# Putting off small-tile visits by a count of TensorE's instructions, and dating layer A's probabilities later, in a two-layer attention kernel

## The chip, the core and the metric

One core of a Trainium2 chip runs the whole program. Its engines work from queues of their own: TensorE (PE, with its weight loads shown apart as PEld), VectorE (DVE), ScalarE (ACT), GpSimd (POOL) and SyncE (SP, here an issuer of DMAs). The metric is device time in microseconds for one execution; lower is better.

## The reference

Two attention layers, A and B, read inputs of 2048 rows by 1024 columns. Each multiplies by `wqkv` (1024 x 3072), attends with 32 heads of 32, and multiplies by `wo` (1024 x 1024); the outputs are put side by side. Only the attention differs.

```python
# A: each row sees 8 keys, two rows apart, itself among them
off = jnp.arange(W) * dil                     # W, dil = 8, 2
idx = pos[:, None] - off[None, :]
logits = jnp.einsum("bhsd,bhswd->bhsw", q, kg) * scale    # kg, vg: k, v gathered at idx
o = jnp.einsum("bhsw,bhswd->bhsd", softmax(where(idx >= 0, logits, -1e9)), vg)
# B: each row sees the last 256 keys
mask = (i - j >= 0) & (i - j < 256)
o = jnp.einsum("bhqk,bhkd->bhqd", softmax(where(mask, q @ k.T * scale, -1e9)), v)
```

## The kernel before

**Units and groups.** The work is eight units of 512 rows: units 0 to 3 are layer B, units 4 to 7 layer A, whose even and odd rows are laid apart so that its eight keys are neighbours. A unit has eight groups of four heads. The 32 groups of layer A are called visits 0 to 31 here; eight of them make a unit.

**Large matmuls.** The projections run on 128-wide tiles. Each fp32 operand is split into a high and a low fp32r part, and three products of parts (`TERMS`) replace one fp32 product. In the profile these are the matmuls `g<-...`: queries and keys (L586), values (L654), the output projection of layer B (L714), and that of layer A (L773), which is done with sums of blocks at the program's end.

**Layer A's small tiles.** A visit has two pieces of TensorE work. `scores` (L923) multiplies 64 pairs of 32x32 and 32x40 tiles into four PSUM banks. `values` (L984) multiplies 16 or 20 tiles of probabilities (`wide`) with values (`vbuf`) into one bank. The operands here are plain fp32, and each such matmul stands in the trace as two weight loads and two matmuls: 64 of them are 256 instructions. A large matmul is two.

**Between them** lies a chain on two other engines: VectorE adds the mask (L931), takes the maximum (L941) and subtracts it (L943); ScalarE takes the exponential (L947); VectorE sums (L955), inverts (L957), multiplies (L959) and turns the tiles (L961); ScalarE spreads them into `wide` (L970, L973, eight copies). Only then can `values` start. After it, ScalarE copies the result out (L1032).

**Loads.** Weights and inputs come through GpSimd's queue (L173) into raw buffers. ScalarE or VectorE makes the high part (L218, L221), VectorE the low part (L224). At the change of a unit the eight tiles of the next input, `x`, are loaded and split in four pairs.

**What sets the order.** Nothing is scheduled on the chip. While the program is built, a planner keeps a clock (`Clock`) with times for all engines and DMAs. There are four lists of work: `aux`, `twos` (values), `ones` (scores) and `gemm` (large matmuls, three at a time, in a fixed sequence). At each step the planner asks the next item of each list when it will be ready, takes the earliest, and emits it. Every engine's order follows from this, for the work that follows a TensorE item is emitted at the time at which the planner thinks it due. The chip then runs each engine's queue strictly in that order.

An item of `values` is ready when its `v` is, when a PSUM bank is, and when `h["p"]`, the planned end of the last copy into `wide`, has come:

```python
return latest(done["v"].get((u, vp)), h.get("p"), ro.when())
```

## Time and profile before

| | |
|---|---|
| median of 3 runs | 1819.04 us (1817.57 to 1820.43) |
| the profiled execution | 1818.1 us, of which the span is 1816.4 us |
| TensorE matmuls busy | 1789.4 us, 99% of the span, 14730 matmuls |
| VectorE, ScalarE, GpSimd busy | 1262.0, 924.4 and 410.1 us |
| layer A's `scores` (L923) | 43.3 us busy |
| layer A's `values` (L984) | 38.5 us busy |
| granted TensorE clock, mean | 0.995 of full speed |

A row of the timeline gives the start in us from the span's start, the length, engine, line, operation, tiles and count; in brackets is the idle time just before it and what ended that. "issue" means that the profile shows nothing that the engine waited for. The length of a run of matmuls ends with the modelled end of the last one, which overlaps the next start by about 0.07 us; differences of starts are the safer measure.

### The profile page before, as it was taken

The numbers are of one execution on the slowest core, as the hardware profiler recorded it, in microseconds if no ns is written. First come the engines' busy times: TensorE is split into PE (matmuls) and PEld (weight loads), VectorE is DVE, ScalarE is ACT, GpSimd is POOL, SyncE is SP. The second block draws the span as 40 slices with busy tenths as digits, with TensorE's granted clock in tenths as the row PEclk, the third lists the DMA queues.
The fourth block names the chain that finished last, engine by engine and source line by source line (L and its number), as shares of the span: only waits on it lengthen the run. The fifth ranks groups of instructions, "written<-read, shape, count | busy, mean of one in ns | idle before, by whom it ended". The sixth has DMA issues, their size and how long they took to land.

```text
span 1816.4 us, 38617 instructions
## 1 busy us (share of the span) xinstructions
PE 1789.4 (99%) x14730; PEld 1465.3 (81%) x14730; DVE 1262.0 (69%) x2790; ACT 924.4 (51%) x2301; POOL 410.1 (23%) x950
## 2 busy tenths in 40 slices
PE   9999999999999999999999999999999999999999
PEld 6787878888777788778887788888888887888887
DVE  6677876768867769777677566646755766557866
ACT  5556466555655565656555344423542544446342
POOL 2313323222242223333224300101010011002220
PEclk9999999999999999999999999999999999999999
DMA  7354664544646555454545343536753674348984
GB/s 239 114 142 136 183 168 139 167 139 137 183 139 177 146 144 170 134 166 128 160 110 164 106 150 119 164 123 213 249 173 113 221 250 137 120 144 297 311 265 145
DMA packets 129241, 303.61 MB, mean 167 GB/s; under 512 B 16160, under 2 KB 31520, under 8 KB 129056
## 3 DMA queue, kind: packets, MB, share of 16 engines
q0 software_dynamic: 45216, 164.65, 28.7%
q1 hardware_dynamic: 73472, 116.56, 22.8%
q10 hardware_dynamic: 10368, 19.93, 3.0%
q8 instruction: 117, 1.92, 0.4%
q14 instruction: 68, 0.56, 0.1%
HBM read 189.79 MB, written 44.04 MB: 129 GB/s over the span
## 4 chain that ended last, share of the span: by engine, by line
PE 91%; DMA 3%; ACT 2%; DVE 2%; issue 1%; SPq 0%; POOL 0%; ACTq 0%; DVEq 0%; POOLq 0%
PE g L586 37%; PE g L654 18%; PE g L714 10%; PE g L773 8%; PE s L1172 5%; PE s L1089 5%; PE o L1219 5%; PE s L923 2%; PE o L984 2%; DMA r<-od 2%; DMA raw<-xs 1%; ACT wide L970 1%; ACT s L1099 0%; DVE w L224 0%; DVE r L846 0%
## 5 line engine op out<-in xcount | busy, mean ns | idle before, releaser
L586 PE MATMUL g<-x,w 128*128 128x512 f32 x3072 | 773.0, 396 | 2.8 <-ACT x L218 2.6
L586 PEld LDWEIGHTS g<-x,w 128*128 128x128 f32 x3072 | 568.1, 189 | 114.5 <-issue 6.8
L654 PE MATMUL g<-w,x 128*128 128x256 f32 (+1 forms) x2304 | 393.7, 322 | 0.5 <-issue 0.3
L224 DVE TENSOR_TENSOR w<-raw,w 128x512 fp32r<-128x512 f32 x518 | 339.4, 697 | 51.8 <-ACT w L218 45.1
L654 PEld LDWEIGHTS g<-w,x 128*128 128x128 f32 x2304 | 334.5, 192 | 28.8 <-issue 1.6
L1099 ACT ACTIVATE s<-s,nm 128x384 f32<-128x384 f32 (+2 forms) x512 | 274.4, 537 | 101.8 <-DVE nm L1094 101.6
L1094 DVE CUSTOM_DVE_ANT_0 s<-s,mask_d 128x384 f32<-128x384 f32 (+2 forms) x512 | 261.7, 554 | 88.1 <-PE s L1089 87.4
L1158 POOL TENSOR_SCALAR_AFFINE_SELECT pbuf<-pbuf 128x128 f32<-128x128 f32 (+1 forms) x606 | 220.1, 391 | 326.2 <-ACT pbuf L1179 324.8
L1179 ACT ACTIVATE pbuf<-s 128x384 f32<-128x384 f32 (+2 forms) x480 | 202.8, 505 | 73.7 <-PE s L1172 72.1
L714 PE MATMUL g<-r,w 128*128 128x512 f32 x768 | 190.8, 394 | 1.4 <-ACT r L1054 0.7
L173 POOL DMA_DIRECT2D raw<-wqk x126 | 68.6, 545 | 440.8 <-DVE w L224 303.0
L714 PEld LDWEIGHTS g<-r,w 128*128 128x128 f32 x768 | 141.9, 188 | 30.7 <-DVE r L1058 1.6
L773 PE MATMUL g<-x,w 128*128 128x512 f32 x672 | 153.2, 390 | 0.5 <-DVE w L224 0.5
L773 PEld LDWEIGHTS g<-x,w 128*128 128x128 f32 x672 | 126.0, 188 | 27.3 <-DVE w L224 0.9
L221 DVE CAST w<-raw 128x1024 fp32r<-128x1024 f32 x187 | 129.3, 692 | 25.2 <-PE g L586 22.6
L1172 PEld LDWEIGHTS s<-qst,kst 128*128 128x128 f32 x704 | 113.3, 189 | 40.6 <-ACT s L1099 16.2
L1089 PE MATMUL s<-kst,qst 96*128 96x384 f32 (+2 forms) x512 | 142.5, 342 | 0.9 <-ACT s L1099 0.7
L1172 PE MATMUL s<-qst,kst 128*128 128x256 f32 (+2 forms) x704 | 136.4, 302 | 3.5 <-ACT s L1099 3.0
L1089 PEld LDWEIGHTS s<-kst,qst 96*128 96x128 f32 x512 | 93.5, 189 | 25.8 <-issue 3.9
L931 DVE TENSOR_TENSOR band<-s,near 128x160 f32<-128x160 f32 x128 | 32.5, 316 | 116.0 <-PE s L923 116.0
L1099 ACT ACTIVATION_READ_ACCUMULATOR s<-s,nm 128x1 f32 x512 | 105.4, 206 | 0.0
L970 ACT COPY wide<-band 32x512 f32<-32x512 f32 x128 | 79.0, 618 | 49.2 <-DVE band L961 47.2
(81 smaller groups left out, 1405.7 us busy)
## 6 DMA issues: line engine op xcount, KB each, us to landing
raw<-wqk POOLq DMA_DIRECT2D x126, 512.0 KB, 4.3
raw<-wv POOLq DMA_DIRECT2D x72, 512.0 KB, 4.9
qst<-nat SPq DMA_DIRECT2D x96, 256.0 KB, 5.4
kst<-nat SPq DMA_DIRECT2D x96, 256.0 KB, 5.5
raw<-wo POOLq DMA_DIRECT2D x44, 512.0 KB, 4.4
raw<-xs POOLq DMA_DIRECT2D x28, 512.0 KB, 4.5
outs<-ost ACTq DMA_DIRECT2D x37, 256.0 KB, 2.8
kst<-halo SPq DMA_DIRECT2D x72, 128.0 KB, 4.4
```

The lines of the kernel that those rows point to most:

```text
L221: nc.vector.tensor_copy(t[:, 0, :], raw)
L224: nc.vector.tensor_tensor(t[:, 1, c:c + 512], raw[:, c:c + 512], t[:, 0, c:c + 512].bitcast(F32), op=ALU.subtract)
L586: nc.tensor.matmul(h["ps"], h["w"][:, a, k * P:(k + 1) * P], xt[u][k][:, b, :], start=(k == 0 and i == 0), stop=(k == NK - 1 and i == 2))
L654: nc.tensor.matmul(ps, xt[u][kw * g + k][:, a, p0:p0 + P], h["w"][g][:, c, k], start=(first and t == 0 and half == 0), stop=(last and t == 2),
L714: nc.tensor.matmul(h["ps"], w[:, a, c:c + P], ot[u, k][:, b, :], start=(k == 0 and i == 0), stop=(k == NK - 1 and i == 2))
L773: nc.tensor.matmul(h["ps"], w[:, a, c:c + P], x[:, b, :], start=(k == 0 and t == 0), stop=(k == 3 and t == 2))
L1089: nc.tensor.matmul(ps[:, :n], q[0:96, j, b * P:(b + 1) * P], kk[0:96, j, c0:c1], start=True, stop=True)
L1094: nc.vector.tensor_tensor_reduce(ps[:, :n], ps[:, :n], mask[:, cut:full], scale=-1.0, scalar=BIG, op0=ALU.add, op1=ALU.min, accum_out=nm)
L1099: nc.scalar.activation(ps[:, :n], ps[:, :n], AF.Exp, bias=nm, scale=-1.0, accum_out=sm)
L1158: nc.gpsimd.affine_select(w, w, pattern=[[0, m], [step, n]], compare_op=ALU.is_ge, fill=0.0, base=base, channel_multiplier=chan)
L1172: nc.tensor.matmul(ps[:, i * n:(i + 1) * n], kk[:, j, 256 + kb * P:256 + (kb + 1) * P], q[:, j, q0:q0 + n], start=True, stop=True)
L1179: nc.scalar.activation(w, ps[:, :pack * n].rearrange("p (j n) -> p j n", j=pack), AF.Exp)
```

## The change

It has two parts, and both act only in the planner.

**The count.** A helper `mm` wraps each matmul and adds 4 (fp32) or 2 to a count of TensorE's instructions. Each time the count passes another 256, at an offset of 150, it notes the planner's time. It takes this as the moment at which TensorE asks for its next 256 instructions. `EXTRA` and `EACH` stand for instructions that the wrapped calls don't show. `short(n)` is true if an item of n instructions would run past the 290 that are still there at the asking, and less than 7.0 us of planned time have passed since. In the main loop an item of `scores` (256 instructions) or `values` (16 to 80) for which this holds is passed over for large matmuls, if those are ready within 0.2 us.

**The date.** The end of layer A's probabilities, `h["p"]`, is taken as 1.5 us later when the planner asks whether `values` is ready.

No work is added or removed. Where the planner finds ScalarE or VectorE free at another time, it hands a piece to the other: nine high parts of weights (L218) go from ScalarE to VectorE (L221), two high parts of inputs and three copies out of PSUM the other way. All matmuls now have one source line, L269, so tile names tell them apart.

```diff
+CHUNK, ASKED, LEFT, FETCHED = 256, 150, 290, 7.0
+EXTRA, EACH = 246, 5.2
+P_LATE = 1.5
...
+    issued, asked = [0.0], [0, 0.0]
+
+    def mm(out, left, right, **k):
+        issued[0] += 4 if left.dtype == F32 else 2
+        n = int(issued[0] + EXTRA - ASKED) // CHUNK
+        if n > asked[0]:
+            asked[:] = n, ck.now
+        nc.tensor.matmul(out, left, right, **k)
+
+    def short(n):
+        return ck.now < asked[1] + FETCHED and issued[0] + EXTRA + n > asked[0] * CHUNK + ASKED + LEFT
...
         def scores():
             qk = rows[hg]
+            issued[0] += EACH
...
-                        nc.tensor.matmul(banks[j][0][32 * i:32 * i + 32, 40 * b:40 * b + 40],
+                        mm(banks[j][0][32 * i:32 * i + 32, 40 * b:40 * b + 40],
...
-            return latest(done["v"].get((u, vp)), h.get("p"), ro.when())
+            return latest(done["v"].get((u, vp)), h.get("p") and h["p"] + P_LATE, ro.when())
...
-        return [Item(scores_ready, scores, CW)], [Item(values_ready, values, C3 + 0.9)]
+        return [Item(scores_ready, scores, CW, 256)], [Item(values_ready, values, C3 + 0.9, 16 * len(kbs))]
...
-        best = None
+        best, other = None, None
         left = False
         for name, seq in seqs.items():
...
             t = seq[pos[name]].ready()
+            if t is not None and name == "g" and t <= ck.now + 0.2:
+                other = max(t, ck.now), name
             if t is not None and (best is None or max(t, ck.now) < best[0]):
                 best = max(t, ck.now), name
+        if best and other and seqs[best[1]][pos[best[1]]].n and short(seqs[best[1]][pos[best[1]]].n):
+            best = other
```

TensorE's order is the same up to the first `scores` visit of layer A, 1043 us into the span, and in the closing run of large matmuls. In between, the places of the 32 `scores` and 32 `values` among the large matmuls move; the large matmuls keep their sequence.

**Place one: TensorE in unit 4, from the `scores` of visit 6 to the `values` of visit 7** (`s<-pbuf` is `scores`, `o<-wide,vbuf` is `values`, `g` the large matmuls). Before:

```order
L923 MATMUL s<-pbuf 32x40 x64
L586 MATMUL g<-x,w 128x512 x6
L654 MATMUL g<-w,x 128x256 x78
L923 MATMUL s<-pbuf 32x40 x64
L654 MATMUL g<-w,x 128x256 x18
L586 MATMUL g<-x,w 128x512 x21
L984 MATMUL o<-wide,vbuf_125 32x136 x12
L984 MATMUL o<-wide,vbuf_125 32x128 x4
L586 MATMUL g<-x,w 128x512 x27
L654 MATMUL g<-w,x 128x512 x9
L984 MATMUL o<-wide,vbuf_125 32x136 x12
```

After:

```order
L269 MATMUL s<-pbuf 32x40 x64
L269 MATMUL g<-x,w 128x512 x6
L269 MATMUL g<-w,x 128x256 x96
L269 MATMUL g<-x,w 128x512 x6
L269 MATMUL s<-pbuf 32x40 x64
L269 MATMUL g<-x,w 128x512 x18
L269 MATMUL o<-wide,vbuf_125 32x136 x12
L269 MATMUL o<-wide,vbuf_125 32x128 x4
L269 MATMUL g<-x,w 128x512 x24
L269 MATMUL g<-w,x 128x512 x15
L269 MATMUL o<-wide,vbuf_125 32x136 x12
```

The `scores` of visit 7 stand 24 large matmuls later; the `values` of visit 6 three later, those of visit 7 six later.

**Place two: TensorE in unit 7, from the `scores` of visit 27 to the `values` of visit 27.** Before:

```order
L923 MATMUL s<-pbuf 32x40 x64
L984 MATMUL o<-wide,vbuf_123 32x8 x4
L984 MATMUL o<-wide,vbuf_123 32x136 x12
L984 MATMUL o<-wide,vbuf_123 32x128 x4
L586 MATMUL g<-x,w 128x512 x48
L923 MATMUL s<-pbuf 32x40 x64
L984 MATMUL o<-wide,vbuf_123 32x8 x4
L984 MATMUL o<-wide,vbuf_123 32x136 x12
L984 MATMUL o<-wide,vbuf_123 32x128 x4
```

After:

```order
L269 MATMUL s<-pbuf 32x40 x64
L269 MATMUL o<-wide,vbuf_123 32x8 x4
L269 MATMUL o<-wide,vbuf_123 32x136 x12
L269 MATMUL o<-wide,vbuf_123 32x128 x4
L269 MATMUL g<-x,w 128x512 x30
L269 MATMUL s<-pbuf 32x40 x64
L269 MATMUL g<-x,w 128x512 x18
L269 MATMUL g<-w,x 128x256 x6
L269 MATMUL o<-wide,vbuf_123 32x8 x4
L269 MATMUL o<-wide,vbuf_123 32x136 x12
L269 MATMUL o<-wide,vbuf_123 32x128 x4
```

The second `scores` of the piece (visit 28) and the `values` of visit 27, which followed each other at once, are now 24 large matmuls apart.

**Place three: VectorE in unit 6, the chain of visit 22** (`w` and `x` are low parts of weights and inputs). Before:

```order
L931 TENSOR_TENSOR band<-s,near 128x4x40 x4
L224 TENSOR_TENSOR w<-raw,w 128x512 x4
L224 TENSOR_TENSOR x<-raw,x 128x512 x2
L941 TENSOR_REDUCE nm<-band 128x16
L943 TENSOR_TENSOR band<-band,nm 128x16x40
L224 TENSOR_TENSOR x<-raw,x 128x512 x6
L955 TENSOR_REDUCE sm<-band 128x16
L957 RECIPROCAL sm<-sm 128x16
L959 TENSOR_TENSOR band<-band,sm 128x16x40
L961 STREAM_TRANSPOSE band<-band 128x1024
```

After:

```order
L946 TENSOR_TENSOR band<-s,near 128x4x40 x4
L507 MEMSET nat 128x8
L956 TENSOR_REDUCE nm<-band 128x16
L958 TENSOR_TENSOR band<-band,nm 128x16x40
L227 TENSOR_TENSOR w<-raw,w 128x512 x4
L227 TENSOR_TENSOR x<-raw,x 128x512 x4
L970 TENSOR_REDUCE sm<-band 128x16
L972 RECIPROCAL sm<-sm 128x16
L974 TENSOR_TENSOR band<-band,sm 128x16x40
L976 STREAM_TRANSPOSE band<-band 128x1024
L227 TENSOR_TENSOR x<-raw,x 128x512 x4
```

The sums of visit 22 no longer stand behind all four pairs of `x`, but behind two.

More of the change, by code (lines that the diff above doesn't have):

```diff
@@ L454, with __init__ @@
     class Item:
-        def __init__(self, ready, run, cost):
-            self.ready, self.run, self.cost = ready, run, cost
+        def __init__(self, ready, run, cost, n=0):
+            self.ready, self.run, self.cost, self.n = ready, run, cost, n
     def latest(*ts):
@@ L713, in run @@
             for i, (a, b) in enumerate(TERMS):
-                nc.tensor.matmul(h["ps"], w[:, a, c:c + P], ot[u, k][:, b, :],
+                mm(h["ps"], w[:, a, c:c + P], ot[u, k][:, b, :],
                                  start=(k == 0 and i == 0), stop=(k == NK - 1 and i == 2))
@@ L772, in run @@
             for t, (a, b) in enumerate(TERMS):
-                nc.tensor.matmul(h["ps"], w[:, a, c:c + P], x[:, b, :], start=(k == 0 and t == 0),
+                mm(h["ps"], w[:, a, c:c + P], x[:, b, :], start=(k == 0 and t == 0),
                                  stop=(k == 3 and t == 2))
@@ L1088, in first @@
             ps, bank = rs.take()
-            nc.tensor.matmul(ps[:, :n], q[0:96, j, b * P:(b + 1) * P], kk[0:96, j, c0:c1],
+            mm(ps[:, :n], q[0:96, j, b * P:(b + 1) * P], kk[0:96, j, c0:c1],
                              start=True, stop=True)
@@ L1127, in rows @@
             ps, bank = rs.take()
-            nc.tensor.matmul(ps[0:32, 0:P], hl.rearrange("p a b -> p (a b)"), cst["ident"], start=True, stop=True)
+            mm(ps[0:32, 0:P], hl.rearrange("p a b -> p (a b)"), cst["ident"], start=True, stop=True)
             def spread():
@@ L1218, in values @@
                 for j in range(4):
[L1219 removed]
+                    mm(h["o"][32 * j:32 * j + 32, q0:q0 + n],
                                      v[:, slot, vc + 32 * j:vc + 32 * j + 32], pbuf[:, j, at[ki]:at[ki] + n],
@@ L1239, in attention @@
             two.append(Item(lambda ks=ks: values_ready(ks), lambda ks=ks: values(ks),
-                            C3 + sum(kbs[k][2] / 592 for k in ks)))
+                            C3 + sum(kbs[k][2] / 592 for k in ks), 16 * len(ks)))
         return one, two
@@ L1279 @@
         for i in range(WARM):
-            nc.tensor.matmul(ps, idle[:, :P], idle, start=True, stop=True)
+            mm(ps, idle[:, :P], idle, start=True, stop=True)
         ck.free["pe"] = 0.6 + 0.43 * WARM
```

9 lines of the change are left out of this document (4 added, 5 removed).

## The prediction

> **What bounds the kernel now.** I read the page's head and its DMA queues first.
>
> ```profile
> span 1816.4 us, 38617 instructions
> PE 1789.4 (99%) x14730; PEld 1465.3 (81%) x14730; DVE 1262.0 (69%) x2790; ACT 924.4 (51%) x2301; POOL 410.1 (23%) x950
> q8 instruction: 117, 1.92, 0.4%
> ```
>
> TensorE is busy for 99%. Whatever moves the time must be one of its few gaps, or the length of its own work. Queue q8 carried 117 packets of 1.92 MB / 117 = 16.4 KB, and TensorE ran 14730 matmuls and as many weight loads: one packet for about 252 of its instructions. I take q8 as its instruction fetch, 256 at a time.
>
> Next, TensorE's waits in the stretch that the change touches (1043 to 1676 us), all six:
>
> ```profile
> PE o L984 <- ACT wide L973: 3.8, 3, 2.5
> PE o L984 <- issue: 2.6, 1, 2.6
> PE s L923 <- issue: 1.9, 2, 1.4
> PE o L984 <- DVE vbuf L610: 0.9, 1, 0.9
> PE g L773 <- DVE w L224: 0.5, 1, 0.5
> PE g L654 <- issue: 0.3, 1, 0.3
> ```
>
> Nine gaps, 10.0 us, of two kinds: 4.8 us in which nothing is waited for (four times), and 5.2 us for data. The timeline of TensorE shows the first kind; a clean visit stands ahead of it:
>
> ```profile
> 1143.02 1.32 PE L923 MATMUL s<-pbuf 32*32 32x40 f32 x128
> 1144.26 1.67 PE L586 MATMUL g<-x,w 128*128 128x512 f32 x6
> 1145.77 9.52 PE L654 MATMUL g<-w,x 128*128 128x256 f32 x78
> 1155.22 1.28 PE L923 MATMUL s<-pbuf 32*32 32x40 f32 x124
> 1157.92 0.26 PE L923 MATMUL s<-pbuf 32*32 32x40 f32 x4 [1.41 <-issue]
> 1158.11 2.42 PE L654 MATMUL g<-w,x 128*128 128x256 f32 x18
> ...
> 1594.89 1.32 PE L923 MATMUL s<-pbuf 32*32 32x40 f32 x128
> 1596.14 0.95 PE L984 MATMUL o<-wide,vbuf 128*32 128x8 f32 x29
> 1599.64 0.64 PE L984 MATMUL o<-wide,vbuf 128*32 128x136 f32 x11 [2.55 <-issue]
> ```
>
> A `scores` visit issues 256 instructions, a whole packet, in 1.24 us (1143.02 to 1144.26). The 78 large matmuls that follow, 156 instructions, take 9.45 us. Visit 7 stops four matmuls before its end, in the midst of independent work, and lasts 2.89 us (1155.22 to 1158.11) instead of 1.24. At 1596 a visit of 256 instructions and one of 80 follow each other, and the second stops for 2.55 us. The DMA view of 1597.0 to 1600.3 us holds
>
> ```profile
> q8 instruction: 1, 0.02, 1.7%
> ```
>
> while 1584 to 1597 us has no q8 row: the packet starts only after the stop. The trace so shows TensorE out of instructions. The clock, in stretches of 5 us after four gaps:
>
> ```profile
> 1155.00:1160.00 5.00, 3.59 (x146) 3.26 (x145) 4.90 (x8) 2.43 (x6) 0.53 (x1) 1.00 0.59 224
> 1340.00:1345.00 5.00, 3.91 (x52) 2.91 (x51) 4.29 (x9) 3.67 (x9) 1.03 (x2) 1.00 0.61 213
> 1500.00:1505.00 5.00, 4.12 (x39) 3.23 (x40) 4.14 (x7) 3.67 (x6) 0.70 (x1) 0.66 0.35 116
> 1600.00:1605.00 5.00, 5.00 (x28) 4.22 (x23) 0.24 (x1) 2.59 (x5) 0.00 (x0) 0.66 0.03 7
> ```
>
> After gaps of 1.41 and 1.09 us it stays at 1.00; after 2.54 and 2.55 us it falls to 0.66, which costs (1 - 0.66) x 5 = 1.7 us each time. The Trainium skill (TensorE: Matmul & The Clock Gate, part 1) has the gate close after an idle window of about 3.4 us. By that, neither gap would close it, and the sum below would lose 2 x 1.7 us; the two rows at 0.66 decide against it.
>
> **The change, part by part.** It moves TensorE's work and adds none, so I sum the gaps that go, those that come, and the cost of the moving itself. A gap's bracket is counted 0.2 us short, since the modelled end of the matmul before covers that much (2.89 - 1.24 = 1.65 against 1.41); I add 0.2 for each.
>
> *Instruction gaps.* In the new order visit 7 comes 6 + 96 + 6 large matmuls, 216 instructions, after visit 6, not 168, and 24 matmuls later (place one); that is 24 x 0.12 us and more for the packet to come. At place two the two visits are parted by 24 large matmuls. The third gap of this kind (0.53 us, visit 23) is parted likewise: 9 + 96 + 3 matmuls instead of 84. The fourth stays:
>
> ```profile
> 1117.18 0.39 PE L654 MATMUL g<-w,x 128*128 128x256 f32 x1
> 1117.92 2.20 PE L654 MATMUL g<-w,x 128*128 128x256 f32 x17 [0.35 <-issue]
> ```
>
> Here the large matmul behind visit 5 waits, and the rule asks only whether the visit itself fits; the visit even moves six matmuls forward. Removed: 2.6 + 1.9 + 3 x 0.2 = 5.1 us, and one fall of the clock, 1.7: **6.8 us**.
>
> Gaps of this kind can come anew, since the rule goes by planned times and a guessed 7 us. Nothing in the trace prices a visit that the rule has placed. The bounds are none, and one of each size seen (0.5 + 1.6 + 2.8 + 1.7 = 6.6 us). I take one of the middle size, **1.6 us** lost, because the planner holds off every visit that it counts short.
>
> *Data gaps.* The rows:
>
> ```profile
> 1174.93 1.12 PE L984 MATMUL o<-wide,vbuf 128*32 128x136 f32 x32 [0.18 <-ACT wide L973]
> 1343.38 1.12 PE L984 MATMUL o<-wide,vbuf 128*32 128x136 f32 x32 [1.09 <-ACT wide L973]
> 1500.88 1.50 PE L984 MATMUL o<-wide,vbuf 128*32 128x136 f32 x32 [2.54 <-ACT wide L973]
> 1656.81 0.66 PE L984 MATMUL o<-wide,vbuf 128*32 128x136 f32 x16 [0.90 <-DVE vbuf L610]
> 1658.61 1.66 PE L773 MATMUL g<-x,w 128*128 128x512 f32 x6 [0.48 <-DVE w L224]
> ```
>
> The largest, visit 22, is VectorE's:
>
> ```profile
> 1487.58 1.29 DVE L224 TENSOR_TENSOR x<-raw,x 128x512 fp32r<-128x512 f32 x2 [2.29 <-ACT x L218]
> 1490.85 1.29 DVE L224 TENSOR_TENSOR x<-raw,x 128x512 fp32r<-128x512 f32 x2 [1.98 <-ACT x L218]
> 1492.52 1.29 DVE L224 TENSOR_TENSOR x<-raw,x 128x512 fp32r<-128x512 f32 x2 [0.38 <-ACT x L218]
> 1493.73 0.81 DVE L955 TENSOR_REDUCE sm<-band 128x16 f32<-128x640 f32 x1
> ```
>
> Its sums stand behind the last pair of `x`, 1493.81. In the new order (place three) they follow the second pair, whose work ends at 1487.58 + 1.29 = 1488.87, so 4.9 us sooner. What is late next is ScalarE, which splits the last pairs before it spreads the tiles; even if that gives 2 us back, the gap of 2.54 is covered. I count 2.7 + 1.7 for the clock = 4.4 us.
>
> For the others the test is the new distance from `scores` to `values` in TensorE's own work, at 0.227 us for a 512-wide and 0.121 for a 256-wide large matmul (9.45 / 78), and 0.21 for an interruption. The first and the last of these prices are from the timeline and from the chain of waits:
>
> ```profile
> 1398.43 11.17 PE L586 MATMUL g<-x,w 128*128 128x512 f32 x48
> 1409.54 1.43 PE L923 MATMUL s<-pbuf 32*32 32x40 f32 x128
> ```
>
> ```profile
> 1673.40 138.98 PE g L773 x612
> ```
>
> where 138.98 / 612 = 0.227, and 11.11 - 48 x 0.227 = 0.21. In visit 14 (1343.38) the distance grows by 1.4 us, six 512-wide matmuls, against a gap of 1.3: 1.2 gained. Visit 7's 0.4 goes if its chain begins sooner, which I expect: its mask no longer stands behind the late pairs of `x`. Visit 6 loses. Its last tile and its `values`:
>
> ```profile
> 1164.58 0.29 ACT L973 COPY wide<-band 32x128 f32<-32x128 f32 x1
> ...
> 1165.24 1.12 PE L984 MATMUL o<-wide,vbuf 128*32 128x136 f32 x32
> ```
>
> The tiles were ready 1164.87 - 1143.02 = 21.9 us after its `scores` began; the `values` came after 22.2, of which 1.65 were visit 7's stop. Without that, the new distance is 1.25 + 1.25 + 30 x 0.227 + 96 x 0.121 + 2 x 0.21 = 21.3, so a gap of 0.6 comes. Near the end (1656.81) VectorE now does one pair of `x` before the block sums instead of behind them, and the `values` come sooner after their `scores`; of 1.1 + 0.7 us I expect 0.4 to go and the rest to pass to the wait for `w`. Sum: 4.4 + 1.2 + 0.4 + 0.4 - 0.6 = **5.8 us**. The bounds are 5.2 + 5 x 0.2 + 1.7 = 7.9 and, if each wait returns, nothing; the second rival goes below that.
>
> *Interruptions.* In TensorE's order a run of large matmuls is broken 59 times by small tiles in this stretch, before 54 times: 5 x 0.21 = **1.1 us** lost.
>
> *What is hidden.* Nine weight splits go from ScalarE (51% busy) to VectorE (69%), and cost nothing as long as the large matmuls find their weights split; if that cover goes, the wait is of the kind of the 0.48 us at 1658.61. GpSimd's queue keeps its order, SyncE's changes only among stores and block sums; the last `values` comes 3 us later ahead of 139 us of closing matmuls, of which only the second half uses its unit's block sums.
>
> Sum: 6.8 - 1.6 + 5.8 - 1.1 = 9.9 us. The profiled execution took 1818.1, so 1808.2; the median before stands 0.9 higher, which gives **1809.1 us**.
>
> **Rivals.**
>
> *The stops at "issue" are no fetches.* If something that the order doesn't touch stops TensorE there, the 6.8 us stay and the order gains 5.8 - 1.1 = 4.7 us: 1814.3. For it: the profile names no cause, and q8 takes only 0.4% of the DMA engines' time. Against: one packet's instructions go in 1.24 us, and the packet of 1597 starts behind the stop. Chance 0.12. The Trainium skill (Runtime: NRT & Kernel Launch, instruction fetch mechanics) agrees on blocks of 256 instructions, but gives TensorE room for 2048 and calls the crossing of a block mostly hidden. By that rule this rival's time would come out; the rows at 1155 and 1596 speak against it.
>
> *The chains stay as long and the `values` wait.* Slower than before. Four visits (7, 19, 23, 30) have `scores` put off by more than their `values`, which now stand 0.7 to 2.2 us nearer. Visit 7: its tiles came 1174.93 - 1155.22 - 1.65 = 18.1 us after the start; the new distance is 1.25 + 57 x 0.227 + 1.05 + 0.42 = 15.7 (1.05 for the `values` between: the 1.12 of its row less the overlap). If the chain isn't shorter, TensorE waits 2.4 us and the clock falls, 4.1 in all. Four of these are 16.4 us against a gain of 9.9: 6.5 slower, 1825.5. It decides from three such waits on. Against: VectorE's late splits lie ahead of these chains, and putting the visit off lets them finish. Chance 0.08.
>
> *Half of it comes back*: two or three new stops for instructions with a fall of the clock, or two such chains. Gain 2 to 4 us, about 1816. Chance 0.16.
>
> **How the numbers follow.** The forecast (1805 to 1813) has 0.64. Best case: all gaps gone, 6.8 + 0.5 + 7.9 - 1.1 = 14.1, so 1804.9. The range goes from there to the third rival, **1804.9 to 1817.0**. A measurement of this kernel tells about 0.2% (3.6 us) from no change. Below 1815.4 lie the forecast, the first rival and a third of the third one: 0.81. Within 0.2% lies the rest of the third: 0.11. Slower: 0.08.
>
> **What would show it.** The "issue" waits of `scores` and `values` fall from 4.5 us to under 2, and the clock shows no stretch at 0.66 near visits 22 and 28. The 0.3 us behind visit 5 remains. Visit 22 has no wait for `wide`; visit 6 gets one of some 0.5 us. I am wrong if TensorE stops for "issue" at new places, if waits for `wide` grow beyond 4 us, or if large matmuls begin to wait for weights.

## The result, and the profile after

The changed kernel takes 1814.04 us (median of 16 runs, 1810.64 to 1817.53) against 1818.76 us of the kernel before in the same comparison: a ratio of 0.9977, with a 95% interval of 0.9967 to 0.9986, so 4.7 us faster. I had forecast 1809.1 us, 9.9 us faster. The profiled execution took 1813.28 us, with a span of 1811.5 us. Single executions of one kernel differ by some 3 to 5 us either way, so one trace tells where time goes, and medians tell how much. Two more comparisons of the same two kernels gave ratios of 0.9996 and 0.9984 (among the experiments). The changed kernel's median was steady, 1814.0, 1814.4 and 1814.2; that of the kernel before was 1818.8, 1815.4 and 1816.9, and 1816.3 and 1816.1 beside two further groups of runs. With the runs of all five comparisons pooled, over several chips, the kernel before has a median of 1816.3 us (136 runs) and the changed kernel one of 1814.2 (40 runs): 2.1 us, ratio 0.9988 (0.9981 to 0.9994, by drawing the single runs anew). So 4.7 us is the upper edge of what was measured, and the gain is more likely near 2 to 3 us.

The view of TensorE's waits in the stretch of layer A (1043 to 1676 us), total, times and longest:

```profile
PE g L269 <- DVE w L227: 4.4, 2, 3.9
PE o L269 <- ACT wide L988: 0.6, 2, 0.4
...
PE g L269 <- issue: 0.2, 1, 0.2
```

Before, "issue" had 4.8 us here and the tiles `wide` 3.8; now they have 0.2 and 0.6. In their place stands one line that was small before: a large matmul waits 3.9 us for a weight. TensorE's timeline shows the cured visits 7, 22 and 28, and then the new place, in unit 6 behind the `scores` of visit 21:

```profile
1158.26 1.31 PE L269 MATMUL s<-pbuf 32*32 32x40 f32 x128
...
1453.76 10.27 PE L269 MATMUL g<-x,w 128*128 128x512 f32 x44
1467.94 6.24 PE L269 MATMUL g<-x,w 128*128 128x512 f32 x19 [3.91 <-DVE w L227]
...
1501.43 1.12 PE L269 MATMUL o<-wide,vbuf 128*32 128x136 f32 x32
...
1597.77 1.18 PE L269 MATMUL o<-wide,vbuf 128*32 128x8 f32 x40
```

Visit 7's `scores` pass in one piece (1.31 us; 2.89 before), visit 22's `values` have no bracket any more (2.54 before), and the `values` near 1597 run in one piece where they stopped for 2.55 us. From the 44th to the 45th matmul behind visit 21, 4.30 us pass. The clock behind it, in stretches of 5 us (the eighth figure is TensorE's granted clock):

```profile
1465.00:1470.00 5.00, 2.06 (x7) 1.69 (x8) 4.90 (x9) 2.48 (x6) 0.53 (x1) 0.92 0.86 310
1470.00:1475.00 5.00, 5.00 (x45) 3.79 (x43) 4.86 (x8) 1.18 (x3) 0.53 (x1) 0.73 0.85 250
```

That costs some (0.08 + 0.27) x 5 = 1.75 us more. The reason stands on VectorE, in the changed kernel:

```profile
1461.29 2.87 DVE L860 TENSOR_TENSOR r<-r 128x512 f32<-128x512 f32 x4 [4.74 <-DMA r<-od]
...
1467.24 1.25 DVE L227 TENSOR_TENSOR w<-raw,w 128x512 fp32r<-128x512 f32 x2
```

and in the kernel before:

```profile
1456.38 1.29 DVE L224 TENSOR_TENSOR w<-raw,w 128x512 fp32r<-128x512 f32 x2
1457.59 2.87 DVE L846 TENSOR_TENSOR r<-r 128x512 f32<-128x512 f32 x4
```

The four operations of a block sum (`r<-r`, background work for the closing products) now stand ahead of the low part of the weight that TensorE needs next, and they wait 4.74 us for the two re-reads of `od`. SyncE's queue tells why those are late. In the changed kernel:

```profile
1448.48 0.88 SPq L866 DMA_DIRECT2D sd<-r  x2
1449.41 2.19 SPq L855 DMA_DIRECT2D r<-od  x2
```

and before:

```profile
1444.95 1.36 SPq L841 DMA_DIRECT2D r<-od  x2
1451.39 0.88 SPq L852 DMA_DIRECT2D sd<-r  x2
```

The stores of one block sum wait for VectorE until 1448.48, and the reads of the next are now queued behind them instead of ahead: 4.5 us later. They also take longer, 9.1 us from issue to landing (median of the two) where the two took 7.7 before.

To set the traces against each other I took, for each matmul, the time since the start of the one before, less the median of that time for the same pair of shapes over all the traces, and added it up by stretch. The last column is the best version found, described below.

| TensorE's lost time, us | before | changed, three executions | block sums moved, two |
|---|---|---|---|
| 1100 to 1160 (visits 5, 7) | 5.9 | 4.2, 3.9, 3.9 | 4.1, 4.0 |
| 1450 to 1480 (visit 21) | 2.1 | 7.7, 8.7, 8.7 | 2.2, 1.7 |
| 1480 to 1510 (visits 22, 23) | 6.0 | 1.5, 1.7, 2.4 | 3.8, 3.7 |
| 1570 to 1630 (visits 27, 28) | 8.4 | 4.9, 4.9, 4.9 | 4.5, 4.1 |
| 1630 to 1660 | 3.5 | 3.8, 4.1, 7.1 | 6.1, 4.0 |
| all from 1036 on | 51.7 | 47.1, 48.1, 52.7 | 46.1, 42.5 |

The kernel before has one column because only one execution of it was traced. The three stretches that I had named win (5.9 - 4.2) + (6.0 - 1.5) + (8.4 - 4.9) = 9.7 us in the first trace, and the one that I had not named loses 5.6; in the other two executions it loses 6.6 and 6.5.

### The profile page after: what moved, and what is told of

The parts are those of the page before. It is cut to its first block, busy times and chain, and to the rows that moved or that the text cites. A ratio compares the mean times of both kernels' runs of the same rounds, so it can differ in the third digit from the quotient of the medians.

```text
span 1811.5 us, 38626 instructions
## 1 busy us (share of the span) xinstructions
PE 1788.4 (99%) x14730; PEld 1461.1 (81%) x14730; DVE 1265.9 (70%) x2794; ACT 918.4 (51%) x2297; POOL 410.0 (23%) x950
## 5 line engine op out<-in xcount | busy, mean ns | idle before, releaser
L269 PE MATMUL g<-x,w 128*128 128x512 f32 x3744 | 927.1, 394 | 7.5 <-DVE w L227 4.6
L269 PEld LDWEIGHTS g<-x,w 128*128 128x128 f32 x3744 | 692.8, 189 | 145.6 <-issue 6.6
L269 PE MATMUL g<-w,x 128*128 128x256 f32 (+1 forms) x2304 | 391.4, 320 | 0.4 <-DVE w L227 0.2
L269 PEld LDWEIGHTS g<-w,x 128*128 128x128 f32 x2304 | 332.3, 190 | 28.5 <-issue 1.7
L269 PE MATMUL g<-r,w 128*128 128x512 f32 x768 | 191.5, 394 | 1.5 <-ACT r L1069 0.7
L269 PEld LDWEIGHTS g<-r,w 128*128 128x128 f32 x768 | 141.8, 188 | 31.3 <-DVE r L1073 1.6
L224 DVE CAST w<-raw 128x1024 fp32r<-128x1024 f32 x196 | 135.6, 692 | 32.7 <-PE g L269 29.5
L269 PEld LDWEIGHTS s<-qst,kst 128*128 128x128 f32 x704 | 113.1, 188 | 40.8 <-ACT s L1114 16.3
L269 PE MATMUL s<-kst,qst 96*128 96x384 f32 (+2 forms) x512 | 142.6, 342 | 1.0 <-ACT s L1114 0.6
L269 PE MATMUL s<-qst,kst 128*128 128x256 f32 (+2 forms) x704 | 136.5, 302 | 3.5 <-ACT s L1114 3.0
L269 PEld LDWEIGHTS s<-kst,qst 96*128 96x128 f32 x512 | 93.4, 189 | 26.1 <-issue 4.4
L176 POOL DMA_DIRECT2D raw<-wv x72 | 45.9, 638 | 237.5 <-DVE w L227 155.8
L269 PE MATMUL o<-pbuf,vbuf 128*32 128x384 f32 (+2 forms) x1408 | 92.2, 391 | 0.0
```

Source lines behind the costliest of these rows:

```text
L176: (self.nc.scalar if early else self.nc.gpsimd).dma_start(raw if len(ap.shape) == 2 else raw.rearrange("p (a b) -> p a b", a=2), ap)
L224: nc.vector.tensor_copy(t[:, 0, :], raw)
L269: nc.tensor.matmul(out, left, right, **k)
```

## The experiments

Theory A at the outset: stops for instructions are cured as forecast, and the missing 5 to 6 us are the one new wait at visit 21. Rival B: the stops were worth less than I said. Rival N: what is called "issue" is no fetch of instructions.

### Taking the wait away in one queue

The reads of the third block sum ahead of the stores of the second, on SyncE alone:

```diff
         for c, ap in loads:
             nc.sync.dma_start(t[c // 2], ap)
             e = ck.copy("load", ck.now)
+        if who == (DU, 2):
+            held_stores.pop()()
...
-            for z in range(2):
-                nc.sync.dma_start(dst[:, 2 * z:2 * z + 2, :], t[z])
+            def stores():
+                for z in range(2):
+                    nc.sync.dma_start(dst[:, 2 * z:2 * z + 2, :], t[z])
+
+            if who == (DU, 1):
+                held_stores.append(stores)
+            else:
+                stores()
```

> The changed kernel with one difference: on SyncE's queue the two re-reads of `od` for the third block sum of the first pair of units stand ahead of the two stores of the second block sum, as they did before the change (there they were issued at 1444.95 us; after it the first store waits until 1448.48 and the reads come at 1449.41 and 1450.33). Nothing else moves on any engine. Theory A (the missing 5 to 6 us are the one new wait of TensorE for a weight at visit 21, 3.91 us by the releaser, 4.30 us from matmul to matmul, and some 1.75 us at a lower clock behind it): the reads land about 4.5 us sooner, the block sum (2.87 us) starts when VectorE comes to it near 1456.6 instead of 1461.29, the weight's low part is ready near 1463.7, TensorE needs it at 1464.0, so the wait falls to 0 to 0.5 us and the clock between 1465 and 1475 stays above 0.95: 1808 to 1810 us. Theory B (the stops for instructions were worth less than the 6.8 us I put on them, and the wait at visit 21 only takes up time that TensorE would lose later): 1813 to 1815 us, with the time back at a later wait.

Measured: 1813.08 us, ratio to the kernel before 0.9982 (0.9972 to 0.9993); all ratios below are to the kernel before in the same comparison, unless another is named. Its timeline of TensorE:

```profile
1465.44 4.64 PE L269 MATMUL g<-x,w 128*128 128x512 f32 x19 [1.00 <-DVE w L227]
...
1476.31 0.23 PE L269 MATMUL s<-pbuf 32*32 32x40 f32 x2 [0.87 <-DMA pbuf<-nat]
```

The reads came at 1448.04, not at 1445; the wait for the weight fell from 3.91 to 1.00 and the clock stayed at 1.00, but the time did not fall to the 1808 to 1810 us that theory A expects (the changed kernel, not run beside it here, has 1814.0 to 1814.4): the `scores` of visit 22 now wait for their copied rows, and smaller waits follow to 1651. So theory A, that this wait is the whole of the missing time, falls.

The other way: on VectorE alone, the block sum behind the weight.

```diff
             end = ck.use("dve", 0.61, r, port=True)
+        while self.late:
+            self.late.pop()()
...
-            for to, x, y, op in ops:
-                nc.vector.tensor_tensor(*[t[c // 2][:, c % 2, :] for c in (to, x, y)], op=op)
+            def sums():
+                for to, x, y, op in ops:
+                    nc.vector.tensor_tensor(*[t[c // 2][:, c % 2, :] for c in (to, x, y)], op=op)
+
+            for _ in ops:
                 e = ck.use("dve", 0.64, ck.now, port=True)
+            if who == (DU, 2):
+                st.late.append(sums)
+            else:
+                sums()
```

> The changed kernel with one difference: on VectorE the four operations of that same block sum (2.87 us, they wait 4.74 us for the re-read of `od`) stand behind the low part of the next weight instead of five rows ahead of it. SyncE's order is the changed kernel's, the reads still land near 1461.2. Theory A: the row sums of the band follow the subtraction as soon as ScalarE's exponential is there (1459.54), the transposition ends near 1462.8, the weight's low part near 1464.1, TensorE waits 0 to 0.5 us at 1464 instead of 4.30, the clock stays up: 1808 to 1810.5 us, the same as with the reads moved. If the two differ, it is the read's own lateness that costs something elsewhere. Theory B: 1813 to 1815 us.

Measured: 1813.26 us, ratio 0.9984 (0.9971 to 0.9996). TensorE's waits, its timeline behind visit 21, and SyncE's queue in this kernel:

```profile
PE s L273 <- DMA pbuf<-nat: 4.8, 5, 2.4
```

```profile
1456.47 14.57 PE L273 MATMUL g<-x,w 128*128 128x512 f32 x63
...
1479.03 0.23 PE L273 MATMUL s<-pbuf 32*32 32x40 f32 x2 [2.44 <-DMA pbuf<-nat]
```

```profile
1463.99 1.24 SPq L859 DMA_DIRECT2D r<-od  x2
1469.50 1.68 SPq L877 DMA_DIRECT2D sd<-r  x2
1471.29 5.88 SPq L524 DMA_DIRECT2D pbuf<-nat  x8
```

All 63 matmuls run through without a wait for the weight. But the later the block sum, the later its store (1469.50), and behind the store on SyncE stand the eight copies of rows that visit 22 needs: 2.44 us of TensorE. So the block sum holds TensorE on two queues, by the weight behind it on VectorE and by the copies behind its store on SyncE. Mending one leaves the other. That explains these two runs; it is tested below.

### Shifting the packets of instructions

Tiny idle matmuls behind the warming ones at the program's start shift the stream of instructions against its packets of 256, with the order of everything else unchanged. 63 of them in the kernel before:

```diff
             nc.tensor.matmul(ps, idle[:, :P], idle, start=True, stop=True)
+        one = idle.bitcast(F32)
+        for i in range(63):
+            r = i % 4
+            nc.tensor.matmul(ps[32 * r:32 * r + 32, 0:40], one[0:32, 0:32], one[0:32, 32:72],
+                             start=True, stop=True)
```

> The kernel before, its order unchanged on every engine, with 63 idle tiny matmuls (32x32 by 32x40, four instructions each, 252 in all) behind the warming ones at the program's start, where TensorE waits 2.57 us for the first x at 11.21 anyway. They shift the whole stream of instructions against the packets of 256. If the stops named issue are packets that come late (theory F), those at 1156.3 (1.61 us), 1490.2 (0.73) and 1596.8 (2.83) go, since the stretch from the asking for a packet to its first instruction, worked out from the starts of before's instructions, becomes 4.7 us or longer there; the shortest stretches are then 2.7 us at 1411 and 4.0 at 1118 and 1655, which may bring back 0.5 to 2 us. With the clock's 1.7 us behind 1597: 1812 to 1815 us. If the stops belong to what the visits do and not to the packets (rival N), they stay where they are and the time stays at 1818 to 1820 us.

Measured: 1817.26 us, ratio 1.0007 (0.9996 to 1.0018), and stops at both of the main places still. My expectation was badly worked out: 252 is 4 short of a whole packet, so it shifts the ends by four instructions only, and the stretches I had measured contained the stops themselves. The rows are worth having all the same:

```profile
1152.76 1.30 PE L923 MATMUL s<-pbuf 32*32 32x40 f32 x126
1157.15 0.26 PE L923 MATMUL s<-pbuf 32*32 32x40 f32 x2 [3.09 <-issue]
...
1594.16 0.96 PE L984 MATMUL o<-wide,vbuf 128*32 128x8 f32 x31
1597.41 0.49 PE L984 MATMUL o<-wide,vbuf 128*32 128x136 f32 x9 [2.29 <-issue]
```

Before, the pieces were 124 + 4 and 29 + 11. One tiny matmul is four instructions, two loads and two matmuls, which the trace shows as two of its x. Both stops moved by exactly that, to the place where the counted instruction is again the 193rd of its packet (give or take one, counting from the start the weight loads, the matmuls and the queue's own instructions that the trace holds). A cause inside the visits would have stayed with the same matmul. The transfers on q8 say the same more directly: in the traces of all the runs, TensorE stops for "issue" 35 times from 1036 us on, and each time it goes on 1.2 to 1.6 us after a packet on q8 has landed (in the kernel before, landed at 1598.07, on at 1599.64).

42 of them (168 instructions) in the changed kernel, whose planner doesn't know of them:

> The changed kernel, its order unchanged, with 42 idle tiny matmuls (168 instructions) at the start which the count in the planner does not know of. Theory F: the same order loses its cover, since the visits now stand across other packets' ends; worked out from the changed kernel's starts, the stretches from asking to need become 1.8 us at 1584, 2.0 at 1436, 2.8 at 1652, 3.4 at 1064, 3.6 at 1106 and 4.0 at 1453, so TensorE stops there for some 1 to 3 us each, named issue; the stops at 1436 and 1453 are taken up in part by the wait for the weight at 1464. 1818 to 1824 us. Rival N: 1813 to 1815 us and no new stops.

Measured: 1815.89 us, ratio 0.9998 (0.9986 to 1.0009). Waits and two places of the timeline:

```profile
PE o L269 <- issue: 3.1, 3, 1.5
PE s L269 <- DMA pbuf<-nat: 2.3, 2, 1.9
```

```profile
1435.99 0.61 PE L269 MATMUL o<-wide,vbuf 128*32 128x136 f32 x10 [1.47 <-issue]
...
1584.01 0.65 PE L269 MATMUL o<-wide,vbuf 128*32 128x136 f32 x13 [1.19 <-issue]
```

The same order stops at five of the six places worked out (not at 1106, but at 1495, where the profile names VectorE), each time at the 193rd of a packet, mostly for shorter times than I said, and the 1818 to 1824 us that I expected did not come. Two of the stops lie ahead of the wait for the weight, which shrank to 0.16 us. Rival N falls; what the stops are worth in time needs a kernel without that wait.

### The two halves of the change

The count alone (`P_LATE` at 0), and the later date alone (`short` returning False):

```diff
-P_LATE = 1.5
+P_LATE = 0.0
```

> The count of instructions alone: the changed kernel with P_LATE at 0, so that the probabilities of layer A are taken for ready when they were before. By my sum the stops for instructions (5.1 us, 1.7 us of lower clock, less 1.6 for new ones) belong to this part: no long stop named issue, a gain of some 4 to 5 us less 1 for interruptions; waits for `wide` of 2 to 4 us remain. If the parts add up: ratio 0.998 to 0.9985. On VectorE visit 21's weight is split ahead of the block sum, as before the change, so the wait of 4.3 us at 1464 should not be there.

```diff
-        return ck.now < asked[1] + FETCHED and issued[0] + EXTRA + n > asked[0] * CHUNK + ASKED + LEFT
+        return False and ck.now < asked[1] + FETCHED and issued[0] + EXTRA + n > asked[0] * CHUNK + ASKED + LEFT
```

> The later date alone: the changed kernel with the count switched off. By my sum the waits for `wide` (4.4 + 1.2 + 0.4 + 0.4 - 0.6 = 5.8 us) go with this part, and the stops for instructions stay at some visits, 3 to 6 us in all, with one fall of the clock. On VectorE the block sum stands ahead of visit 21's weight as in the changed kernel, so a wait of some 4 us is to be expected there too, unless a stop for instructions ahead of it takes its place. If the parts add up: ratio 0.9985 to 1.000.

Measured: the count alone 1812.95 us, ratio 0.9984 (0.9974 to 0.9995); the date alone 1815.66 us, ratio 0.9998 (0.9985 to 1.0012). The timeline of the count alone, and then that of the date alone:

```profile
1157.41 2.83 PE L269 MATMUL g<-w,x 128*128 128x256 f32 x15 [2.72 <-DVE band L946]
```

```profile
1467.10 3.31 PE L269 MATMUL g<-x,w 128*128 128x512 f32 x9 [2.94 <-DVE w L227]
...
1598.46 1.04 PE L269 MATMUL o<-wide,vbuf 128*32 128x136 f32 x10 [2.50 <-issue]
```

The count alone has no wait at visit 21, as expected, and no stop named issue above 0.2 us, but one of 2.72 us behind visit 7's `scores`. The trace puts it down to VectorE's masking, which ended 0.4 us before TensorE went on; it is also the 193rd instruction of a packet, and a packet on q8 landed 1.6 us before TensorE went on, as at the stops named issue. So this is in all likelihood a late packet too, which the count alone did not avoid. The date alone has what it was expected to have: visit 21's wait, and the old stop near 1597 with 2.50 us. So the date brings the block sum ahead of the weight, and the count wins the stops. The date by itself gains nothing that is clear of noise. The intervals leave open whether the two gains add up.

### Moving the block sums away

If transfers and queues of the four block sums at 1420 to 1480 are what holds TensorE there (theory C, below), they can go elsewhere. First by asking for them 95 us later and letting the planner do the rest, in the changed kernel and in the kernel before:

```diff
-                        output_sums(DU, s - 1)
+                        ck.defer(ck.now + 95.0, lambda: output_sums(DU, s - 1))
```

> The changed kernel, with the first pair's four block sums (eight re-reads of `od`, eight stores of `sd`, sixteen operations of VectorE) asked for 95 us later, in the stretch from 1515 us on, where the DMA engines are busy for 0.34 to 0.46 of the time, instead of 1420 to 1480, where they are at 0.59, 0.95 and 0.70. Some rows of TensorE's order shift with it by a few large matmuls. Theory C (formed on the two runs before: the wait at visit 21 went, and 1.2, 0.9, 0.8 and 0.4 us came back at 1475, 1500, 1635 and 1651 as waits for seat copies and weights, so that from visit 21 on transfers and the chains behind them set TensorE's place): with the load taken out of the dense stretch the waits at 1464, 1475 and 1500 go together, some 4 to 6 us; the ones after 1630 stay, since the second pair's sums stay there. 1809 to 1812 us against 1813 to 1814 of the changed kernel, that is a ratio of 0.995 to 0.9965. Rival D (it is the chain of the visit itself, copies on ScalarE and the issuing on SyncE, and not the load): the waits at 1475 and 1500 stay and the time is that of the changed kernel, ratio 0.997 to 0.9985.

> The kernel before with the same block sums asked for 95 us later, as a control: what the load costs without the change. Theory C: the kernel before lost nothing to the block sums in this stretch that a timeline shows (its stops there are for instructions and for visit 22's tiles, whose sums stand behind pairs of `x`), so no more than 1 to 2 us, a ratio of 0.999 to 1.000; the gain of the delay belongs to the change's order. If the block sums cost the kernel before as much as the changed one (ratio 0.995 to 0.998), the conflict was there all along and the change did not bring it. Where the planner's order moves, a stop for instructions may come or go: 0.5 to 2.8 us each way.

Measured: in the changed kernel 1814.07 us, ratio 0.9986 (0.9975 to 0.9997); in the kernel before 1821.31 us, ratio 1.0027 (1.0014 to 1.0041). Of the first, the timeline:

```profile
1450.68 15.27 PE L269 MATMUL g<-x,w 128*128 128x512 f32 x66
...
1494.69 1.14 PE L269 MATMUL g<-x,w 128*128 128x512 f32 x3 [1.45 <-DVE w L224]
...
1575.55 0.19 PE L269 MATMUL s<-pbuf 32*32 32x40 f32 x1 [1.58 <-issue]
```

Both gaps near 1464 and 1476 are gone (lost time from 1450 to 1480: 1.5 us), but the planner made another order behind them, with a new wait for a weight and new stops for instructions, and theory C's 1809 to 1812 us did not come. The control shows the same in the kernel before, whose timeline has

```profile
1543.26 3.18 PE L586 MATMUL g<-x,w 128*128 128x512 f32 x8 [2.90 <-DVE w L224]
```

and, among its stops for instructions, two of 3.2 and 1.6 us; it is slower than either expectation for it. A new plan is a new draw; neither run prices the block sums. So I moved them by hand, behind the planner's back, with TensorE's, ScalarE's and GpSimd's orders unchanged to the word, again in both kernels:

```diff
+        if key == "s" and who[0] == DU:
+            first_sums[who[1]] = issue
+            issue = lambda part: None
...
             qk = rows[hg]
+            n = hg - 55
+            if 0 < n < 5:
+                first_sums[n - 1]("add")
+                first_sums[n - 1]("store")
+            if 0 <= n < 4:
+                first_sums[n]("load")
```

(`issue` holds the reads, the four operations or the stores of one block sum; the inserted lines stand at the start of `scores`.) Beside them ran the changed kernel itself, and the moved one with the 42 tiny matmuls:

> The changed kernel as it is, beside the next three on the same chip, so that they can be set against it and not only against the kernel before. Ratio to the kernel before 0.9967 to 0.9986, TensorE's wait for the weight of visit 21 near 1464 again some 3 to 4.5 us.

> The changed kernel, TensorE's, ScalarE's and GpSimd's orders word for word the same; only the first pair's four block sums are moved, by hand and behind the planner's back: their reads of `od`, VectorE's 16 operations and the stores of `sd` stand ahead of the scores of visits 23 to 27 (1495 to 1582 us) instead of between 1420 and 1480. Against the run before with the sums asked for 95 us later, nothing else is replanned, so no new stops for instructions by another order. Theory C (transfers and VectorE's work of the block sums at 1440 to 1480 hold up visit 21's weight and, behind it, visit 22's seat copies): the losses of TensorE between 1450 and 1480, 7.7 us in the changed kernel and 5.2 with the reads moved, fall to some 1.7; 5 to 6 us less than the changed kernel, ratio to it 0.9967 to 0.9973. Rival D (as soon as TensorE is earlier, later waits for seat copies, weights and instructions take it back): less than 3 us, ratio to the changed kernel 0.9985 or more, with the time back behind 1480.

> The control: the kernel before with the same block sums moved in the same way, TensorE's order unchanged. Theory C as it stands against my forecast (the change brought the conflict): no more than 1 us, ratio to the kernel before 0.9995 to 1.0005. If the block sums held up the kernel before too, a gain of 2 to 5 us: 0.997 to 0.999, and then the conflict was there, with the stops of visits 22 and 28 around it.

> The changed kernel with the block sums moved, and 42 idle tiny matmuls (168 instructions) at the start, as in the run with the shifted packets, to price stops for instructions where no wait behind them takes them up. That run showed them at 1062 (0.8 us), 1434 (1.7), 1454 (0.7), 1495 (0.7), 1582 (1.5) and 1653 (0.7), 6.1 us. If a stop for instructions moves the end by its own length (as my sum took it), this is 5 to 6 us longer than the kernel with the sums moved, ratio to it 1.0027 to 1.0033. If what TensorE loses there is made up by waits that shrink later, 0 to 3 us, ratio up to 1.0017.

Measured against the kernel before: the changed kernel 1814.40 us, 0.9996 (0.9984 to 1.0007); the block sums moved 1811.29 us, 0.9978 (0.9968 to 0.9987); the kernel before with them moved 1819.54 us, 1.0020 (1.0009 to 1.0031); the moved one with shifted packets 1817.42 us, 1.0009 (0.9998 to 1.0020).

The moved version against the changed kernel: 1811.29 / 1814.40 = 0.9983 (0.9973 to 0.9997, by drawing the single runs anew), 3.1 us. Its timeline:

```profile
1452.33 14.58 PE L269 MATMUL g<-x,w 128*128 128x512 f32 x63
...
1472.20 1.31 PE L269 MATMUL s<-pbuf 32*32 32x40 f32 x128
...
1495.68 1.12 PE L269 MATMUL o<-wide,vbuf 128*32 128x136 f32 x32 [0.98 <-ACT wide L1009]
...
1648.34 0.29 PE L269 MATMUL s<-pbuf 32*32 32x40 f32 x13 [1.89 <-issue]
```

Both holds are gone together: no wait for the weight, none for visit 22's rows, and 8.7 - 2.2 = 6.5 us less lost between 1450 and 1480. This shows the block sums, on the two queues, as the cause of that stretch. But only 3.1 us reach the end, which lies between theory C (5 to 6 us) and rival D (less than 3), and the interval reaches to both. Visit 22's `scores` now start 7 us sooner (1472.20 against 1479.47) and its tiles come late, and 1.9 us stop for instructions at 1648. ScalarE in this kernel shows what visit 22's tiles wait for:

```profile
1486.15 1.14 ACT L221 CAST x<-raw 128x512 fp32r<-128x512 f32 x2 [5.98 <-DMA raw<-xs]
```

The last unit's `x` lands at 1486, and ScalarE and VectorE split it ahead of the visit's own work.

The control, moved in the kernel before, does not gain; it is 4.1 us slower, which neither expectation had. Its timeline has

```profile
1500.01 2.01 PE L1005 MATMUL o<-wide,vbuf 128*32 128x136 f32 x32 [4.23 <-ACT wide L994]
```

where 2.54 us stood. So the block sums did not hold the kernel before at visit 21 (2.1 us lost from 1450 to 1480 with and without the move): the change's order brought that. Why the control is slower is shown only in part: 1.8 us more are lost between 1480 and 1510, and some more in small pieces behind.

The shifted packets in the moved version cost 1817.42 - 1811.29 = 6.1 us (ratio 1.0034, 1.0025 to 1.0045), about what was expected if each stop moves the end by its own length. The stops are not the six of the run before, though: the longest is 3.23 us where that run had 1.47, and others are shorter. By the measure of the table this execution lost 52.0 us and the moved one without shift 46.1. Its timeline and its clock at the longest:

```profile
1439.19 1.04 PE L269 MATMUL o<-wide,vbuf 128*32 128x136 f32 x10 [3.23 <-issue]
...
1586.98 0.65 PE L269 MATMUL o<-wide,vbuf 128*32 128x136 f32 x14 [1.18 <-issue]
```

```profile
1435.00:1440.00 5.00, 1.77 (x43) 1.15 (x33) 4.57 (x10) 0.00 (x0) 0.00 (x0) 0.84 0.53 151
1440.00:1445.00 5.00, 5.00 (x15) 3.97 (x14) 0.00 (x0) 1.18 (x3) 0.53 (x1) 0.50 0.48 161
```

Rival B falls with that: where no wait behind takes them up, stops for instructions and the clock's fall behind them move the end.

### Both once more

> The changed kernel a third time, on whichever chip. If the first comparison holds, the ratio is 0.9967 to 0.9986 and the second (0.9996) was its edge; if the gain is near 0.1%, the ratio is 0.998 to 0.9995 again. In either case the trace shows TensorE's wait for the weight of visit 21 near 1464, 3.5 to 4.5 us with a lower clock behind it, and no stop for instructions above 0.6 us.

> The changed kernel with the first pair's block sums moved by hand, again beside the changed kernel. If what took back half of the wait of visit 21 is bound to the order (visit 22's tiles behind the splits of the last unit's x), a gap of 1 to 2 us stands near 1494 again; if it was the chance of one execution, it does not. The same for the stop of 2.1 us at 1646 named issue, ahead of which the packet was asked for 5.5 us earlier, as long as at 1409 and 1551 where TensorE did not stop for more than 0.6. Ratio to the changed kernel 0.9975 to 0.999 by the first pair of runs; 0.997 or less if the wait of visit 21 passes on whole.

Measured: the changed kernel 1814.24 us, ratio 0.9984 (0.9973 to 0.9994); the moved version 1810.82 us, ratio 0.9966 (0.9951 to 0.9980), which is 0.9981 of the changed kernel (0.9967 to 0.9991), 3.4 us. TensorE's timeline in the changed kernel, and then in the moved version:

```profile
1467.67 4.64 PE L269 MATMUL g<-x,w 128*128 128x512 f32 x10 [4.38 <-DVE w L227]
...
1653.71 0.37 PE L269 MATMUL s<-pbuf 32*32 32x40 f32 x11 [2.17 <-issue]
```

```profile
1494.92 1.12 PE L269 MATMUL o<-wide,vbuf 128*32 128x136 f32 x32 [1.04 <-ACT wide L1009]
```

Visit 21's wait stands in all three executions of the changed kernel (3.91, 3.96 and 4.38 us). Visit 22's tiles are late in both executions of the moved version: that belongs to the order. The stop near 1650 does not: the changed kernel had it here and not in its other two traces, the moved version had it in the first trace and not here. It is the same packet each time; what decides whether it comes in time is not known.

## Why the prediction was right or wrong

Right was that the change is faster (clear of noise in two of three comparisons), that the time lies in the range, and that late packets and visit 22's chain made the gaps; the gain was less than half of the forecast, in part because the forecast put a term at nothing that cost 5.6 us.

- *Instruction gaps, 6.8 us.* Right. They are packets of 256 instructions (that a packet starts only after the stop has begun holds near 1597, at 1597.18; for visit 7 it started at 1154.72 and landed at 1156.51, as TensorE stopped), the stops move with the packets, and they move the end: 6.1 us by the shifted one. Visit 7's stop went, and the one near 1597 went with the clock's fall, though the stretch of visits 27 and 28 gained 3.5 us where the sum had 2.8 + 1.7. What I allowed for new stops (1.6 us) fits the three traces taken together: stops named issue add up to 0.2, 0.4 and 2.6 us, the longest 2.2 us near 1653.
- *Data gaps, 5.8 us.* Right for visit 22, whose stretch gained 4.5, 4.3 and 3.6 us. In the first trace visit 14 kept 0.4 us and visit 6 got a gap of 0.2 us, where I had said 0.6; in the other two neither shows a gap.
- *Interruptions, 1.1 us.* Not tested by itself.
- *What is hidden.* This is the step that failed. I wrote that the work moved to VectorE costs nothing as long as the large matmuls find their weights split, that a wait there would be of the kind of 0.48 us, and that SyncE's order "changes only among stores and block sums". The runs showed in its place 3.9 to 4.4 us of wait at one weight and a lower clock behind it (1.75 us in the first execution): 5.6, 6.6 and 6.5 us more lost in that stretch than before. And it was not the nine splits, but what I passed over in half a sentence: a store ahead of a read on SyncE, and a block sum ahead of a weight on VectorE. I knew that these rows moved, and did not ask what each waits for and what stands behind it.
- *The sum.* 9.9 - 5.6 = 4.3 us, against 4.7, 2.6 and 1.0 measured. Taking both holds away gave 3.1 and 3.4 us; the rest of the 6.5 went in part to visit 22's tiles (2 us in the table, 1480 to 1510), and in part I can't say. That the version without the holds comes to 1811.3 and 1810.8 us, near the 1809.1 of the forecast, is in part luck: I started from 1819.04 us, the median of three runs, and over 136 runs the kernel before has 1816.3. From there the version without the holds gains some 5 us, not 9.9, so about half of the forecast gain is still missing there, and where it goes is open.
- *Rivals.* "No fetches" gave 1814.3, the measured time, by a mechanism that the runs refute: the right number for the wrong reason. Longer chains did not come. "Half of it comes back" had the right spirit, but named new stops for instructions and chains, not a weight. The sign that I had written down as speaking against me, large matmuls that begin to wait for weights, is the one that appeared.

## What to carry to other kernels

When a planner's rows change places only among themselves on an in-order queue, list for each what it waits for, what stands behind it and who needs that: here a store that waits for an adder stood ahead of a read, and the adder's next work ahead of a weight that TensorE needed in 10 us. A wait behind which another queue is held by the same work is not mended by freeing one queue, so move the work itself. With small fp32 tiles at four instructions each, count instructions as well as microseconds, and shift the stream by some tens of instructions to tell a late packet from a late operand.

## What the runs showed of the hardware

A packet of instructions does not always come at the same time. The same packet in the same order cost 1.9 and 2.2 us in two executions and nothing in three others. When TensorE has run dry, it goes on 1.2 to 1.6 us after the packet has landed, in 35 of 35 stops. The Trainium skill (Runtime: NRT & Kernel Launch, instruction fetch mechanics) calls the crossing of a block mostly hidden; here the crossings cost 6.1 us in one kernel and little in another by the position of the blocks alone.

The length of a stop alone does not tell whether TensorE's clock falls. After a wait of 1.9 us for copied rows in the kernel with shifted packets it stayed at 1.00, and after 1.89 us in the version with the block sums moved it fell to 0.97 and 0.69. The rows, first of the one and then of the other:

```profile
1475.00:1480.00 5.00, 3.10 (x134) 2.73 (x135) 1.30 (x6) 0.00 (x0) 0.27 (x1) 1.00 0.81 272
1480.00:1485.00 5.00, 5.00 (x41) 4.84 (x40) 3.63 (x6) 3.98 (x7) 0.41 (x1) 1.00 0.51 184
```

```profile
1645.00:1650.00 5.00, 3.06 (x168) 2.72 (x168) 4.90 (x9) 2.91 (x6) 2.33 (x4) 0.97 0.52 154
1650.00:1655.00 5.00, 5.00 (x16) 3.99 (x16) 4.15 (x9) 2.03 (x4) 1.29 (x3) 0.69 1.00 352
```

The Trainium skill (TensorE: Matmul & The Clock Gate, part 1) has a window that runs free, which fits that equal stops differ; its length of about 3.4 us doesn't fit a fall after 1.89 us.
